# Gated mix of an S5 state space layer and a SiLU feed-forward layer: skip term from natural x, 64-row remainders in alternating order, last state tile in two halves

## The chip, the core and the metric

The kernel runs on one core of a Trainium2 chip. Its time is the device time of one execution in microseconds; the figure that counts is the median of several executions. The engines of the core are named as the profile names them: PE is the matrix engine (PEld its weight loads), DVE the vector engine, ACT the scalar engine, POOL the GpSimd engine, SP the engine that here only issues DMA transfers.

## The reference

With x of shape 2048 x 448 (tokens by channels, bf16):

```
g = sigmoid((x * gate_w).sum(-1))
Bu = x @ B_bar.T                      # complex, B_bar from Lambda, dt, B
h[t] = Lam_bar * h[t-1] + Bu[t]       # 2048 steps, 448 complex states
a = 2 * Re(h @ C.T) + x * Dskip       # the skip term is x * Dskip
b = silu(x @ w1) @ w2                 # 448 -> 1792 -> 448
out = g * a + (1 - g) * b
```

## The kernel before

**Tokens in pairs.** Token 2k is called even, token 2k+1 odd; the 1024 pairs are 8 blocks `kt` of 128. An output tile is 128 tokens of one kind by 448 channels, so there are 16 tiles, numbered `2 * kt + odd`. `XT` holds x transposed (channels on the partitions), for even tokens in its slots 0 to 3 and for odd ones in 4 to 7. 448 channels are three slots of 128 rows and a remainder of 64 rows. `XN` holds x as it lies in memory (tokens on the partitions).

**The matmuls with x.** The feed-forward layer is worked on in four chunks `c` of 512 tokens (`c // 2` is odd, `c % 2` the half of the time axis). `ffn1_mm` takes up to four blocks of 128 hidden channels at a time: for each block three matmuls over the 128-row slots (line 297), and after all blocks of the group one 64-row matmul for each (line 309). The 64-row matmuls lie alternately in the lower and the upper half of the rows, so two run side by side; the half that x isn't in is served by `XR`, a copy of the remainder in the other 64 partitions (`swap_xr`). `bu(pt, h)` does the same for the state inputs of state tile `pt` and time half `h` (lines 625 and 635). ACT takes the results out of the eight PSUM banks, which are given out in turn by `nxt`. `ffn2` (line 597) makes one output tile of the feed-forward layer, and ACT writes it times (1 - g) into the tile's place in `XN` (line 602, `bs`).

**The scan.** 448 complex states are four tiles `pt`; tile 3 holds its 64 states in one slot. `scan(pt)` on DVE combines two tokens into one step (weigh, line 655), turns the phase away by a table of cosines and sines, runs two `tensor_tensor_scan` instructions over 1024 pairs (line 662), turns back, which gives the states of odd tokens in `HS`, and then makes those of even tokens in `VE` (line 655 again). `scan3` does this for tile 3 with DMAs that swap partitions. The tables are made by POOL and DVE (`phases`, `phases2`) and by ACT (`tables`: sine, absolute value, cosine).

**The gate.** `gate` multiplies `XN` in place by a broadcast copy of `gate_w` (DVE, line 563, four instructions of 1792 columns), `gate2` sums each tile on ACT (line 571) and makes the sigmoid.

**The output stage.** `yopen` starts an output tile in a PSUM bank: five matmuls over state slots (line 754), then the skip term: three matmuls of 128 columns of `XT` with the diagonal matrices `DE` (line 756) and one of 64 rows and 64 columns (line 758). `yclose` adds the two slots of state tile 2 (line 774); DVE then multiplies by g and adds the feed-forward part (line 781), and SP stores the tile. All eight odd tiles are opened first, then closed, then the even tiles follow one by one.

**The order.** There is no scheduler. Each engine executes its instructions in the order in which the Python code records them, and `Tracker` puts semaphore waits in front of an instruction for what it reads and overwrites, by names of buffers. POOL also waits for its own previous instruction. The recorded order is the list at the end of the function (lines 805 to 862); a generator such as `s0 = scan(0)` gives its instructions piece by piece at each `run`. On SP, the DMAs stand in a queue in recorded order.

Of the kernel before, what the change touches and what calls it, by code (L numbers as in the profile page):

```python
# [7 lines left out]
ALU = mybir.AluOpType  # L8
AF = mybir.ActivationFunctionType

F32 = DT.float32
# [135 lines left out]
def gated_mix(nc, A_x, A_Lambda_re, A_Lambda_im, A_B_re, A_B_im, A_C_re, A_C_im, A_log_dt,  # L147
              A_Dskip, B_x, B_w1, B_w2, gate_w, out):
    with ExitStack() as ctx:
# [17 lines left out]
        DE = sb("DE", [128, 4, 128], BF16)  # L167
# [7 lines left out]
        OT = [sb(f"OT{i}", [128, D], BF16) for i in range(4)]  # L175
        GWB = sb("GWB", [128, D], BF16)
        JK = sb("JK", [128, 2], BF16)
# [6 lines left out]
        TMPS = [sb(f"TMP{i}", [128, D], F32) for i in range(3)]  # L184
# [4 lines left out]
        SG = sb("SG", [128, 2], F32)  # L189
        HP = sb("HP", [128, 1], F32)  # L190
# [3 lines left out]
        def bs(tile):  # L194
            return XN[:, tile * D:(tile + 1) * D]
# [64 lines left out]

        ldt_odd(0)
        ldt(XT[:, 0:4, 512:1024], x2[512:1024, 0:512], "XTe1")
        ldt_odd(1)
        XC_ALL = ["XC0", "XC1"] + [f"XC3_{q}" for q in range(4)]
# [19 lines left out]

        def ffn1_mm(c, fbs):

            odd, h = c // 2, c % 2
            hs = slice(h * 512, (h + 1) * 512)
            x0 = 4 * odd
            banks = [nxt() for _ in fbs]  # L290
            xk = XO[h] + [f"XR{h}b"] if odd else XE[h] + [f"XR{h}a"]

            for fb, bank in zip(fbs, banks):
                def mm(pe, fb=fb, bank=bank):
                    ins = None
                    for j in range(3):
                        ins = pe.matmul(ps[:, bank, :], W1E[:, j, fb * 128:(fb + 1) * 128],  # L297
                                        XT[:, x0 + j, hs], start=(j == 0), stop=False)
                    return ins
                wk = ["W1Ej0", "W1Ej1", "W1Ej2"] if fb < NFA else ["W1Ed"]  # L300
                T.op("pe", mm, reads=wk + xk, writes=[f"ps{bank}"])

            def rest(pe):
                ins = None
                for i, (fb, bank) in enumerate(zip(fbs, banks)):
                    up = (i % 2 == 1) != bool(odd)
                    p = slice(64, 128) if up else slice(0, 64)
                    x = XT[p, x0 + 3, hs] if up == bool(odd) else XR[p, hs]
                    ins = pe.matmul(ps[:, bank, :], W1E[p, 3, fb * 128:(fb + 1) * 128], x,  # L309
                                    start=False, stop=True)  # L310
                return ins
            T.op("pe", rest, reads=["W1Ea", "W1Ez"] + xk, writes=[f"ps{bank}" for bank in banks])
            return list(zip(fbs, banks))
# [153 lines left out]
        def tmp(m):  # L467
            if m < 4:
                return FP[:, 1 + m // 2, (m % 2) * 512:(m % 2) * 512 + D], f"F{1 + m // 2}"
            return TMPS[m - 4][:, :], f"TMP{m - 4}"  # L470

# [17 lines left out]
        swap_xr("dve", 0, 1)  # L489
        phases2(2)  # L490
        swap_xr("dve", 1, 0)
        swap_xr("dve", 1, 1)
# [57 lines left out]
        def side_diag():  # L550
            for j in range(4):
                T.op("dve", lambda e, j=j: e.tensor_scalar(
                    DE[:, j, :], ID[:, :], PV[:, j, 3:4], None, ALU.mult),
                    reads=["ID", "PV"], writes=[f"DE{j}"])
            yield

        def load_xn():
            ld("sp", XN[:, :].rearrange("p (k c) -> p k c", k=NKT), x2.rearrange("(k p) c -> p k c", p=128), "XN")

        def gate():  # L560
            for b in range(4):
                v = XN[:, 4 * b * D:4 * (b + 1) * D].rearrange("p (k c) -> p k c", k=4)
                T.op("dve", lambda e, v=v: e.tensor_tensor(  # L563
                    v, v, GWB[:, :].unsqueeze(1).to_broadcast([128, 4, D]), ALU.mult),
                    reads=["XN", "GW"], writes=[f"XG{b}"])
                yield

        def gate2():
            for t in range(2 * NKT):
                v = XN[:, t * D:(t + 1) * D]  # L570
                T.op("act", lambda e, t=t, v=v: e.activation(v, v, AF.Copy, accum_out=Z[:, t:t + 1]),  # L571
                     reads=[f"XG{t // 4}"], writes=[f"Z{t}", f"BS{t}"])
# [14 lines left out]
        def ffn2(c, q):  # L587
# [4 lines left out]
            bank = nxt()  # L592

            def mm(pe):
                ins = None
                for fb in range(NFB):
# [7 lines left out]
                 reads=[f"ps{bank}", "GT2"], writes=[f"BS{tile}"])  # L604
# [7 lines left out]
        def bu(pt, h):  # L612
# [7 lines left out]
            for odd, banks in ((0, be), (1, bo)):  # L620
                for m, bank in zip(ms, banks):
                    def mm(pe, m=m, bank=bank, odd=odd):
                        ins = None
                        for j in range(3):
                            ins = pe.matmul(ps[:, bank, :], bt(slice(0, 128), j, m),  # L625
                                            XT[:, 4 * odd + j, hs], start=(j == 0), stop=False)
                        return ins
                    T.op("pe", mm, reads=(["BR"] if pt == 3 else BTK[0:2]) + (XO if odd else XE)[h], writes=[f"ps{bank}"])

            def rest(pe):  # L630
                ins = None
                for m, b0, b1 in zip(ms, be, bo):
                    for odd, bank in ((0, b0), (1, b1)):
                        p = slice(64 * odd, 64 * odd + 64)
                        ins = pe.matmul(ps[:, bank, :], bt(p, 3, m),  # L635
                                        XT[p, 4 * odd + 3, hs], start=False, stop=True)
                return ins
            T.op("pe", rest, reads=(["BR"] if pt == 3 else BTK) + XO[h] + XE[h], writes=[f"ps{b}" for b in be + bo])
# [21 lines left out]
        def sc(c, pt):  # L660
            rb = c1("rr", pt).to_broadcast([128, NK])
            T.op("dve", lambda e: e.tensor_tensor_scan(G[:, c, :], rb, Q1[:, c, :], 0.0, ALU.mult, ALU.add),  # L662
                 reads=[f"Q1{c}", "rr"], writes=[f"G{c}"])

        def scan(pt):
# [6 lines left out]
            hk = [f"HS{a}", f"HS{b}"]  # L672
            cs = COS[:, pt, :].unsqueeze(1).to_broadcast([128, 2, NK])
            sn = SIN[:, pt, :].unsqueeze(1).to_broadcast([128, 2, NK])
            tk = [f"COS{pt}", f"SIN{pt}"]
            lr, li, nli = c1("lr", pt), c1("li", pt), c1("nli", pt)
            lk = ["lr", "li", "nli"]
            parts = [(0, 1), (1, 2)] if pt == 0 else [(0, 2)]
            for h0, h1 in parts:
# [3 lines left out]
                stt(u[:, 1, w], ve[:, 0, w], li, G[:, 1, w], lk + v0[0] + GK, v1[1])  # L683
                yield
            tt(Q1[:, :, :], u, cs, ALU.mult, uk[0] + uk[1] + tk, QA)
            tt(Q2[:, :, :], u, sn, ALU.mult, uk[0] + uk[1] + tk, QB)
            tt(Q1[:, 0, :], Q1[:, 0, :], Q2[:, 1, :], ALU.add, QA + QB, ["Q10"])
            tt(Q1[:, 1, :], Q1[:, 1, :], Q2[:, 0, :], ALU.subtract, QA + QB, ["Q11"])
            sc(0, pt)
            sc(1, pt)  # L690
            yield
            tt(Q1[:, :, :], G[:, :, :], cs, ALU.mult, GK + tk, QA)
            tt(Q2[:, :, :], G[:, :, :], sn, ALU.mult, GK + tk, QB)
            tt(u[:, 0, :], Q1[:, 0, :], Q2[:, 1, :], ALU.subtract, QA + QB, [hk[0]] + uk[0])
# [110 lines left out]
        for fb, bank in first:  # L805
            ffn1_act(0, fb, bank)
# [92 lines left out]
```

## Time and profile before

| what | value |
|---|---|
| median of 5 executions | 152.18 us (151.95 to 152.56) |
| profiled execution: time, span in the trace | 151.95 us, 149.9 us |
| granted PE clock | 1.000 |
| PE busy | 143.9 us (96%), 756 matmuls |
| DVE busy | 119.5 us (80%) |
| ACT busy | 81.8 us (55%) |
| POOL busy | 15.1 us (10%), none of it after 22.4 us |
| DMA | 12.30 MB |

Busy times are sums of the spans of an engine's instructions. A matmul's own span is longer than the distance to the next one, since matmuls are pipelined; its rate is read from the distance between starts. The chain of work that ended last follows the last instruction back to what released it. The timeline merges instructions of one line that follow each other into one row: start, busy time, engine, line, output and inputs, count, and in brackets how long the engine was idle before and what ended that.

### The profile page before, as it was taken

The numbers are of one execution on the slowest core, as the hardware profiler recorded it, in microseconds if no ns is written. First come the engines' busy times: TensorE is split into PE (matmuls) and PEld (weight loads), VectorE is DVE, ScalarE is ACT, GpSimd is POOL, SyncE is SP. The second block draws the span as 40 slices with busy tenths as digits, with TensorE's granted clock in tenths as the row PEclk, the third lists the DMA queues.
The fourth block names the chain that finished last, engine by engine and source line by source line (L and its number), as shares of the span: only waits on it lengthen the run. The fifth ranks groups of instructions, "written<-read, shape, count | busy, mean of one in ns | idle before, by whom it ended". The sixth has DMA issues, their size and how long they took to land.

```text
span 149.9 us, 1958 instructions
## 1 busy us (share of the span) xinstructions
PE 143.9 (96%) x756; PEld 64.8 (43%) x763; DVE 119.5 (80%) x148; ACT 81.8 (55%) x130; POOL 15.1 (10%) x20
## 2 busy tenths in 40 slices
PE   6999899999999999999999999999999999999992
PEld 2443233333354533334554333345555555555550
DVE  1573898719999999999999999999999992196441
ACT  1269969577999996988994556652131300000000
POOL 7039990000000000000000000000000000000000
PEclk9999999999999999999999999999999999999999
DMA  4998797998943003011000000000000000044211
GB/s 130 295 242 193 158 215 141 334 381 220 187 53 85 0 0 70 0 42 33 0 0 0 0 0 0 4 0 0 0 0 0 4 0 0 0 145 162 66 61 61
DMA packets 22976, 12.30 MB, mean 82 GB/s; under 512 B 16180, under 2 KB 22456, under 8 KB 22968
## 3 DMA queue, kind: packets, MB, share of 16 engines
q1 hardware_dynamic: 22388, 11.23, 29.5%
q10 hardware_dynamic: 580, 0.95, 2.2%
q8 instruction: 6, 0.10, 0.3%
q14 instruction: 2, 0.02, 0.0%
HBM read 6.15 MB, written 1.84 MB: 53 GB/s over the span
## 4 chain that ended last, share of the span: by engine, by line
PE 82%; ACT 12%; DMA 2%; issue 1%; DVE 0%
PE ps L597 25%; PE ps L297 16%; PE ps L625 12%; PE ps L754 11%; ACT AT L333 5%; PE ps L774 5%; PE ps L322 3%; PE ps L309 3%; ACT XN L571 3%; PE ps L635 3%; DMA CO<-in_A_x_dram 2%; PE ps L756 2%; ACT COS L461 2%; PE ps L758 1%; ACT SIN L456 1%; PE ps L373 1%
## 5 line engine op out<-in xcount | busy, mean ns | idle before, releaser
L597 PE MATMUL ps<-W,AT 128*128 128x448 bf16 x224 | 43.1, 353 | 0.3 <-ACT AT L333 0.3
L297 PE MATMUL ps<-XT,W1E 128*128 128x512 bf16 x142 | 33.5, 380 | 0.7 <-issue 0.5
L333 ACT ACTIVATE AT<-ps 128x1024 bf16<-128x1024 f32 (+1 forms) x32 | 27.2, 917 | 6.6 <-PE ps L309 6.6
L597 PEld LDWEIGHTS ps<-W,AT 128*128 128x128 bf16 x224 | 21.6, 98 | 21.1 <-ACT AT L333 0.7
L297 PEld LDWEIGHTS ps<-XT,W1E 128*128 128x128 bf16 x147 | 13.2, 98 | 19.8 <-issue 4.4
L781 DVE SCALAR_TENSOR_TENSOR OT<-ps,GT,XN 128x448 bf16<-128x448 f32 x16 | 10.4, 680 | 12.8 <-PE ps L774 12.7
L602 ACT ACTIVATE XN<-ps,GT 128x448 bf16<-128x448 f32 x16 | 9.6, 631 | 16.3 <-PE ps L597 16.3
L625 PE MATMUL ps<-XT,BT 128*128 128x512 bf16 x70 | 16.1, 379 | 0.8 <-ACT AT L333 0.7
L662 DVE TENSOR_TENSOR_SCAN G<-P,Q 128x1024 f32<-128x1024 f32 x6 | 13.4, 2274 | 0.0
L641 ACT ACTIVATE VE<-ps 128x1024 bf16<-128x1024 f32 (+1 forms) x8 | 7.4, 921 | 7.4 <-PE ps L635 7.4
L625 PEld LDWEIGHTS ps<-XT,BT 128*128 128x128 bf16 x72 | 6.7, 97 | 9.9 <-issue 2.0
L571 ACT ACTIVATE XN<-XN 128x448 bf16<-128x448 bf16 x16 | 9.0, 563 | 0.0
L754 PE MATMUL ps<-CO,HS 128*128 128x448 bf16 x40 | 8.9, 354 | 0.0
L754 PE MATMUL ps<-CO,VE 128*128 128x448 bf16 x40 | 8.9, 352 | 0.0
L655 DVE SCALAR_TENSOR_TENSOR HS<-VE,P,G 128x512 bf16<-128x512 bf16 (+1 forms) x8 | 7.8, 1015 | 0.1
L309 PE MATMUL ps<-XT,W1E 64*128 64x512 bf16 x25 | 7.8, 382 | 0.0
L309 PE MATMUL ps<-XR,W1E 64*128 64x512 bf16 x24 | 7.6, 382 | 0.0
L655 DVE SCALAR_TENSOR_TENSOR VE<-HS,P,G 128x1024 bf16<-128x1024 bf16 x6 | 7.4, 1281 | 0.1
L563 DVE TENSOR_TENSOR XN<-XN,GWB 128x1792 bf16<-128x1792 bf16 x4 | 4.1, 1085 | 4.1 <-DMA XN<-in_A_x_dram 4.1
L643 ACT ACTIVATE HS<-ps 128x1024 bf16<-128x1024 f32 (+1 forms) x8 | 7.4, 922 | 0.0
L655 DVE SCALAR_TENSOR_TENSOR G<-VE,P,HS 128x1024 f32<-128x1024 bf16 (+1 forms) x4 | 7.3, 1814 | 0.1
L655 DVE SCALAR_TENSOR_TENSOR G<-HS,P,VE 128x2048 f32<-128x2048 bf16 x3 | 7.0, 2350 | 0.1
(98 smaller groups left out, 167.0 us busy)
## 6 DMA issues: line engine op xcount, KB each, us to landing
XN<-in_A_x_dram SPq DMA_DIRECT2D x1, 1792.0 KB, 9.9
out_dram<-OT SPq DMA_DIRECT2D x16, 112.0 KB, 1.7
W<-in_B_w_dram SPq DMA_DIRECT2D x1, 1568.0 KB, 13.8
W1E<-in_B_w_dram ACTq DMA_DIRECT2D x3, 224.0 KB, 6.0
W1E<-in_B_w_dram SPq DMA_DIRECT2D x1, 672.0 KB, 8.7
HS<-HS SPq DMA_DIRECT2D x4, 128.0 KB, 2.3
W1E<-in_B_w_dram SPq DMA_DIRECT2D x2, 224.0 KB, 4.8
CO<-in_A_x_dram ACTq DMA_DIRECT2D x1, 256.0 KB, 4.0
```

Source lines behind the costliest of these rows:

```text
L297: ins = pe.matmul(ps[:, bank, :], W1E[:, j, fb * 128:(fb + 1) * 128], XT[:, x0 + j, hs], start=(j == 0), stop=False)
L309: ins = pe.matmul(ps[:, bank, :], W1E[p, 3, fb * 128:(fb + 1) * 128], x, start=False, stop=True)
L333: T.op("act", lambda e: e.activation(a[:, fb:fb + n, :], ps[:, bank:bank + n, :], AF.Silu), reads=[f"ps{bank + i}" for i in range(n)], wri ...
L571: T.op("act", lambda e, t=t, v=v: e.activation(v, v, AF.Copy, accum_out=Z[:, t:t + 1]), reads=[f"XG{t // 4}"], writes=[f"Z{t}", f"BS{t}"])
L597: ins = pe.matmul(ps[:, bank, 0:D], a[:, fb, q * 128:(q + 1) * 128], W2[:, fb, :], start=(fb == 0), stop=(fb == NFB - 1))
L602: T.op("act", lambda e: e.activation(bs(tile), ps[:, bank, 0:D], AF.Copy, scale=GT[:, 2, tile:tile + 1]), reads=[f"ps{bank}", "GT2"], writ ...
L625: ins = pe.matmul(ps[:, bank, :], bt(slice(0, 128), j, m), XT[:, 4 * odd + j, hs], start=(j == 0), stop=False)
L655: T.op("dve", lambda e: e.scalar_tensor_tensor(o, a, s, b, ALU.mult, ALU.add), reads=reads, writes=writes)
L662: T.op("dve", lambda e: e.tensor_tensor_scan(G[:, c, :], rb, Q1[:, c, :], 0.0, ALU.mult, ALU.add), reads=[f"Q1{c}", "rr"], writes=[f"G{c}"])
L754: ins = pe.matmul(ps[:, bank, 0:D], state(kt, odd, m), CO[:, m, :], start=(m == 0), stop=False)
L774: ins = pe.matmul(ps[:, bank, 0:D], state(kt, odd, m), CO[:, m, :], start=False, stop=(m == YB[-1]))
L781: T.op("dve", lambda e: e.scalar_tensor_tensor(o[:, :], ps[:, bank, 0:D], GT[:, 1, tile:tile + 1], bs(tile), ALU.mult, ALU.add), reads=[f" ...
```

## The change

1. The skip term is no longer made from `XT` and diagonal matrices. POOL multiplies `XN` in place by `DB`, a broadcast copy of `Dskip` (`skip`, four instructions of 1792 columns), and `yopen` adds the product with one 448-column matmul by the identity matrix. `DE` and `side_diag` go. As `XN` now keeps the product to the end, the gate products go to other buffers (`xg`: parts of `CO`, `OT` and `TMPS`), and the feed-forward parts of the tiles go to parts of `IOTA`, of `FP` and of `BT` (`bs`).
2. `ffn1_mm` and `bu` take the 64-row matmuls last and first in turn (`half`), so that those of two groups stand next to each other. `ffn2` sets the turn back.
3. `scan(2)` runs in two time halves, with 512 pairs to an instruction; the second half starts from the last value of the first. The output stage takes the eight tiles of the first time half to the end, then the other eight; `yout` (the DVE instruction and the store) is recorded apart from `yclose`, between the pieces of the second half of `scan(2)`.
4. Moves: the broadcast load of `gate_w`, and that of `Dskip`, are issued early on ACT's queue; `XN` is loaded in two halves, one before and one after the last transposing loads of x; two of the three remaining `swap_xr` copies go from DVE to POOL, behind the first two skip products; the first table set (`t0`) is recorded behind the rest of the first chunk's evacuations.

```diff
         def bs(tile):
-            return XN[:, tile * D:(tile + 1) * D]
+            kt, odd = tile // 2, tile % 2
+            if odd:
+                return BT[:, :, :].rearrange("p j n -> p (j n)")[:, kt * D:(kt + 1) * D]
+            v = (FP[:, 0, :] if kt > 3 else IOTA[:, :]).bitcast(BF16)
+            return v[:, (kt % 4) * D:(kt % 4 + 1) * D]
...
+        for dst, src, key in ((GWB, gate_w, "GW"), (DB, A_Dskip, "DB")):
+            ld("act", dst[:, :], row(src).partition_broadcast(128).rearrange("p o n -> p (o n)"), key)
         ldt_odd(0)
         ldt(XT[:, 0:4, 512:1024], x2[512:1024, 0:512], "XTe1")
+        load_xn(0)
         ldt_odd(1)
+        load_xn(1)
...
+            for part in (rests, mains) if rf else (mains, rests):
+                part()
+            half[0] = not rf
...
         phases2(1)
-        swap_xr("dve", 0, 1)
         phases2(2)
         swap_xr("dve", 1, 0)
-        swap_xr("dve", 1, 1)
...
+        def skip():
+            for b in range(4):
+                v = XN[:, 4 * b * D:4 * (b + 1) * D].rearrange("p (k c) -> p k c", k=4)
+                T.op("pool", lambda e, v=v: e.tensor_tensor(
+                    v, v, DB[:, :].unsqueeze(1).to_broadcast([128, 4, D]), ALU.mult),
+                    reads=[f"XN{b // 2}", "DB"], writes=[f"XD{b}"])
+                yield
...
-                 reads=[f"ps{bank}", "GT2"], writes=[f"BS{tile}"])
+                 reads=[f"ps{bank}", "GT2"], writes=[f"BS{tile}"] + (bsk(tile) if kt % 4 == 0 and (h == 0 or not odd) else []))
...
+            if cut:
+                for h in range(2):
+                    for f in (weigh, turn, back, even):
+                        f(h, h + 1)
+                        yield
+                return
...
-                for j in range(3):
-                    ins = pe.matmul(ps[:, bank, j * 128:(j + 1) * 128], XT[:, 4 * odd + j, xr], DE[:, j, :],
-                                    start=False, stop=False)
-                return pe.matmul(ps[:, bank, 384:D], XT[p, 4 * odd + 3, xr], DE[p, 3, p], start=False, stop=False)
+                tile = 2 * kt + odd
+                return pe.matmul(ps[:, bank, 0:D], ID[:, :], XN[:, tile * D:(tile + 1) * D], start=False, stop=False)
...
+        run(ffn1(0, NFA))
         run(t0)
-        run(ffn1(0, NFA))
         bu(0, 0)
...
-        run(g1)
+        run(g1, 2)
+        run(g0, 2)
         run(s0, 1)
         run(s3, 2)
+        run(g1)
+        swap_xr("pool", 0, 1)
+        swap_xr("pool", 1, 1)
...
         run(coef)
+        run(g0)
...
-        run(s2)
+        run(s2, 4)
...
+        done = []
+        for kt in range(4):
+            for odd in (1, 0):
+                done.append(yclose(*yopen(kt, odd)))
+        run(s2, 1)
+        yout(*done.pop(0))
+        run(s2, 1)
+        while done[2:]:
+            yout(*done.pop(0))
+        run(s2, 1)
+        while done:
+            yout(*done.pop(0))
+        opened = [yopen(kt, 1) for kt in range(4, 8)]
+        run(s2, 1)
+        for kt in range(4, 8):
+            opened.append(yopen(kt, 0))
+            done.append(yclose(*opened.pop(0)))
+        while opened:
+            done.append(yclose(*opened.pop(0)))
+        while done:
+            yout(*done.pop(0))
```

`weigh`, `turn`, `back` and `even` are the pieces of the old `scan` with bounds `h0, h1` on the time axis; the other scans call them as before. In the second half the scan's initial value is `G[:, c, 511:512]`.

## The prediction

> **What bounds the kernel now.** First the page's slices: PE is busy at 7 to 9 tenths in all but the first and last; DVE has a dip in slice 9 and is nearly free in slices 34 and 35; POOL stops after slice 6.
>
> ```profile
> PE   6999899999999999999999999999999999999992
> ...
> DVE  1573898719999999999999999999999992196441
> ...
> POOL 7039990000000000000000000000000000000000
> ```
>
> Then the chain that ended last: PE has 82% of it, ACT 12%, DVE nothing. PE reaches the output stage at 119.13 and its last matmul ends at 146.98; one DVE instruction and the store follow. So PE bounds it, and DVE has room. How much room the waits and DVE's timeline tell: DVE waits 4.15 us for `XN`, works without a gap from 33.10 to 124.51, and then waits 6.01 us for PE.
>
> ```profile
> 33.10 4.09 DVE L563 TENSOR_TENSOR XN<-XN,GWB 128x1792 bf16<-128x1792 bf16 x4 [4.15 <-DMA XN<-in_A_x_dram]
> ...
> 100.65 2.35 DVE L655 SCALAR_TENSOR_TENSOR G<-VE,P,HS 128x2048 f32<-128x2048 bf16 x1
> ...
> 122.03 2.48 DVE L655 SCALAR_TENSOR_TENSOR VE<-HS,P,G 128x1024 bf16<-128x1024 bf16 x2
> 130.53 5.72 DVE L781 SCALAR_TENSOR_TENSOR OT<-ps,GT,XN 128x448 bf16<-128x448 f32 x9 [6.01 <-PE ps L774]
> ```
>
> **PE: 64-row remainders.** PE's timeline, one group of `ffn1_mm`:
>
> ```profile
> 58.03 2.76 PE L297 MATMUL ps<-XT,W1E 128*128 128x512 bf16 x12
> 60.72 0.39 PE L309 MATMUL ps<-XT,W1E 64*128 64x512 bf16 x1
> ...
> 60.95 0.38 PE L309 MATMUL ps<-XT,W1E 64*128 64x512 bf16 x1
> ...
> 61.26 1.04 PE L297 MATMUL ps<-XT,W1E 128*128 128x512 bf16 x3
> ```
>
> Twelve matmuls take 2.76 us, the last of them 0.38, so they start 0.216 apart. Group to group is 3.23 us for fourteen such steps (12 and two pairs), which make 3.02: each excursion to 64 rows costs 0.21. In the recorded order there are 22 excursions before, 11 after (first chunk 2 to 1; the stage with `bu(0)`, `bu(3)` and `ffn1(1)` 8 to 4; `bu(1)` and `bu(2)` 2 to 1 each; `ffn1(2)` and `ffn1(3)` 4 to 2 each): 11 x 0.21 = 2.3 us.
>
> Up to `bu(1)` at 51.78 five merges lie (1.05). Moving `t0` takes away PE's wait of 0.72 at 19.02, but `ffn1(1)` still waits for the `XR` copy on DVE (behind `phases2`, it ended at 24.06 and should end near 23.9), so of all before it only about 0.2 is kept; three merges follow (0.63), and ACT, released earlier in the group with remainders first, no longer holds the second half of `ffn2(0)` (0.26). So 1.1 there, and six merges later (1.26): PE could begin the output stage at 116.7. A group with remainders first needs its four banks at once; by ACT's timeline each was free before PE comes, the closest the bank of the copies of line 648, free at 26.5 for 27.2.
>
> **PE: skip.**
>
> ```profile
> 119.13 1.11 PE L754 MATMUL ps<-CO,HS 128*128 128x448 bf16 x5
> 120.08 0.33 PE L756 MATMUL ps<-DE,XT 128*128 128x128 bf16 x3
> 120.34 0.20 PE L758 MATMUL ps<-DE,XT 64*128 64x64 bf16 x1
> 120.47 1.12 PE L754 MATMUL ps<-CO,HS 128*128 128x448 bf16 x5
> ```
>
> Skip takes 120.08 to 120.47, 0.40 with the slower start behind it; a 448-column matmul takes 0.19 ((120.08 - 119.13) / 5). 16 x 0.21 = 3.4 us saved. The stage becomes 16 x 8 x 0.19 = 24.3 and would end at 141.0. The last four closes then stand 0.38 apart and DVE needs 0.64 each (5.72 / 9), so its last instruction would end at 142.4, where before it was 147.69: 5.3 us faster, 146.9, were PE all.
>
> **DVE.** `skip` puts POOL beside DVE. What that does the first 21 us show:
>
> ```profile
> 8.23 0.24 DVE L409 TENSOR_TENSOR P<-P,PV 128x4 f32<-128x4 f32 x2 [0.28 <-ACT P L412]
> ...
> 9.91 1.03 DVE L409 TENSOR_TENSOR P<-P 128x4 f32<-128x4 f32 x2
> 12.03 1.23 DVE L451 SCALAR_TENSOR_TENSOR FP<-G,FP 128x1024 f32<-128x1024 f32 x1 [1.09 <-POOL G L446]
> ```
> ```profile
> 9.70 1.16 POOL L444 TENSOR_SCALAR FP<-IOTA,P 128x1024 f32<-128x1024 f32 x1 [5.49 <-DVE P L409]
> 10.95 1.05 POOL L446 TENSOR_SCALAR G<-FP 128x1024 f32<-128x1024 f32 x1
> 12.16 2.08 POOL L444 TENSOR_SCALAR Q<-IOTA,P 128x1024 f32<-128x1024 f32 x1 [0.17 <-POOL G L446]
> ```
>
> Two DVE instructions of four columns, 0.24 elsewhere, take 1.03 and end just behind POOL's instruction from 9.70 (10.86); POOL's at 12.16 takes 2.08 because DVE's at 12.03 is in front. Such instructions exclude each other whole, and POOL gets in after the DVE instruction in progress. Nearly all that DVE does in the scans reads two operands from SBUF as these do, so each product costs DVE its full length.
>
> That length, P, no row shows. Below: the one-operand row, 1.05 us for 1024 columns, scaled to 1792 is 1.83. [...] I take 3.93, since the products have two operands and the row has one. Two 64-row copies of 512 columns move to POOL behind the second product, an estimated 0.53 each by the same row: 1.1.
>
> The sum on DVE. ACT now does the first chunk's evacuations to about 19.2, then `t0` (3.29, from 14.58 to 17.87), so `bu(0,0)` is out at 24.3; DVE's two weighs (2.66 + 1.52, by their starts from 24.77) end at 28.5. Before, they ended at 28.95 and DVE then waited for `XN`; now its first half is loaded ahead of the last transposing loads (issued near 19.3) and there by then. From 33.10 to 100.65, where scan 2 starts, DVE worked 67.55 without a gap; `DE` goes (0.65). So scan 2 starts at 28.5 + 66.9 + 4 x 3.93 + 1.1 = 112.2 instead of 100.65. POOL's first product covers the one wait left (for ACT's evacuation of `bu(0,1)`, near 31.7).
>
> Halves: by the half-size rows (weigh and even 2.66 each, turn 4.45, with scans of 1.15 as half of 2274 ns, back 3.15) one half is 12.9, two are 25.8 instead of 23.9. The first half is done at 125.1, but PE would want it for its second tile near 119.
>
> **What waits for DVE on the way.** `scan3` keeps `FP` slot 0 until its last instruction (71.53 + 1.28 = 72.8 before; now 28.5 + 39.05 + 16.8 = 84.4). ACT must write the results of `ffn2(1)` there; queued behind are the evacuations of `bu(2)`. `bu(2,1)` needs those banks, free at about 86.6, and PE is there at 81.5: 5.1 us of wait, so the output stage starts at 121.8. In it the second tile waits for DVE (125.1), and the eighth is closed at 134.9; DVE does weigh, one output, turn, five, back, two, even: 18.1, to 143.2, without waiting; then eight outputs, 5.1, and 0.3 for PE's last closes: 148.65. Before, this was 147.69: 0.95 later. From there on the store and the end stay (149.9 - 147.7 = 2.2). Span 150.8, execution 151.95 + 0.95 = 152.9, and as the median lies 0.23 above that execution, 153.1.
>
> **Loads.** `gate_w` and `Dskip` are issued on ACT between its table load (ends 4.5) and its next instruction at 7.99: hidden. Their bytes and 0.9 MB of `XN` now precede the last loads of odd x (landed at 23.9 and 24.4), needed by `bu(0,1)` near 27.2. At the 381 GB/s of the slice with the most traffic 1.1 MB are 3 us, so PE may wait 0.3, at worst 2; DVE is behind POOL then, and the end is not moved. `W2` is issued as late as before (23.6) with fewer bytes ahead. ACT's gate sums need the third product with `gate_w` near 44.9; DVE should have it near 44.6.
>
> **Rivals.** (1) *The product is shorter.* The end follows 153.1 + 4 (P - 3.93) until PE sets it, near P = 2.4. It decides at P = 3.7, where the time is that of before; at 3.3 it is 150.6, at the row's 1.83 it is 146.9. For it: POOL's only rows are this fast, the operands are bf16. Against: none has two operands. (2) *PE gets late as well*: groups with remainders first wait for banks, or the loads of odd x slip by 2 us and more; added to the wait at `bu(2,1)` this passes the closes on to the end, 154.5 to 156. For: PE's last close (146.8) is only 1.9 before DVE's end. (3) *The merged remainders save nothing*, if the cost is per pair and not per change of rows: 2.3 us back on PE, of which about 1 reaches the end: 154. Against: between the two pairs above there is only 0.23.
>
> **How the numbers follow.** Main case 46%, 152.0 to 154.2 with P between 3.65 and 4.2; rival 1 36%, 147 to 151.7; rival 2 12%; rival 3 6%. 0.3% (0.46 us) is what a measurement can tell. Main and rival 2 and 3 above 152.64: 0.46; main between 151.72 and 152.64 with rival 1's edge: 0.14; rival 1: 0.40. The range takes in most of rival 1 and half of rival 2: 147.8 to 155.2, and 152.0 to 154.2 for the main case.
>
> **What would show it.** Right: four POOL rows of 3.5 to 4.1 us, DVE rows beside them longer by as much, scan 2 starting near 112, ACT waiting for DVE at its evacuation of `ffn2(1)`, PE waiting near 81 to 87, DVE in the chain's end; fourteen steps to the group with one change of rows; output tiles 1.51 apart. Wrong: DVE rows beside POOL no longer than elsewhere, or scan 2 before 107.

## Result, and the profile after

The changed kernel takes 152.56 us in the median of 22 executions (150.99 to 154.05), the kernel before 152.25 (151.82 to 153.13, 43 executions): the ratio is 1.0005, 95% interval 0.9988 to 1.0022. The forecast was 153.1, slower by 0.6%; measured is no difference. The profiled execution took 151.68 us with a span of 149.7 (before 151.95 and 149.9). Here and below, a ratio and its interval leave out executions more than 1.5% above the fastest of their kernel, while medians and ranges take in all. The changed kernel scatters more than the kernel before, in step with the clock granted to PE: of its 23 executions with the profiled one, the 12 with 0.995 of the clock or more average 152.03, the other 11, with 0.978 to 0.989, 152.85.

The page of the changed kernel, its slices and the engines and lines of the chain that ended last:

```profile
PE   6999959699999999999999799999999998999990
...
DVE  1563785958999999999999999999999999999974
...
POOL 7029990069939920000000000000000000000000
...
DVE 56%; PE 16%; SPq 13%; issue 7%; DMA 5%; ACT 1%; DVEq 0%
```

The bound has changed hands: DVE has 56% of the chain, where PE had 82%. It is not DVE's alone, though: at 124.15 PE waits 0.61 us for DVE, from there on PE works without a gap and the chain is PE's, and near the end DVE waits 0.81 us for PE. The two are nearly tied. (The shares of SPq and DMA lead back from DVE's row at 34.20 to the last loads of x. POOL held that row until 35.53, longer than the loads did; the chain doesn't show that.) DVE's hollow near the end (slices 34 and 35) is gone; PE has new hollows in slices 6 and 8 (18.7 to 22.5 and 26.2 to 29.9 us) and a small one in slice 23. POOL works on to slice 15.

DVE's timeline of the changed kernel:

```profile
29.88 2.21 DVE L585 TENSOR_TENSOR CO<-XN,GWB 128x1792 bf16<-128x1792 bf16 x2
34.20 2.40 DVE L696 SCALAR_TENSOR_TENSOR G<-VE,P,HS 128x1024 f32<-128x1024 bf16 x1 [2.12 <-ACT HS L684]
36.64 4.97 DVE L696 SCALAR_TENSOR_TENSOR HS<-VE,P,G 128x512 bf16<-128x512 bf16 x2
...
45.34 4.60 DVE L693 TENSOR_TENSOR Q<-HS,COS 128x2048 bf16<-128x2048 bf16 x1
49.86 4.60 DVE L693 TENSOR_TENSOR Q<-HS,SIN 128x2048 bf16<-128x2048 bf16 x1
...
110.90 1.28 DVE L696 SCALAR_TENSOR_TENSOR G<-VE,P,HS 128x1024 f32<-128x1024 bf16 x1
...
144.41 0.69 DVE L851 SCALAR_TENSOR_TENSOR OT<-ps,GT,BT 128x448 bf16<-128x448 f32 x1 [0.81 <-PE ps L841]
145.01 2.57 DVE L851 SCALAR_TENSOR_TENSOR OT<-ps,GT,FP 128x448 bf16<-128x448 f32 x4
```

and POOL's over the same stretch:

```profile
31.20 8.85 POOL L593 TENSOR_TENSOR XN<-XN,DB 128x1792 bf16<-128x1792 bf16 x2 [8.41 <-DVE CO L585]
40.19 1.90 POOL L230 COPY XR<-XT 64x512 bf16<-64x512 bf16 x2
44.55 8.82 POOL L593 TENSOR_TENSOR XN<-XN,DB 128x1792 bf16<-128x1792 bf16 x2 [2.47 <-DVE OT L585]
```

Read the two side by side. `Q<-HS,COS` takes 1.22 us where POOL is still; here it and its neighbour take 4.60. The first of them starts at 45.34, while the third product (recorded from 44.55) works, and runs only when that has ended (48.86). A row on either engine contains the wait for the other. So the true length of a product is read from the end of the DVE instruction in front of it to its own end: the first goes from 32.09 (the end of the gate products) to 35.53, 3.44 us; the second from 36.61 (the end of the row at 34.20) to 40.05, again 3.44; the other two likewise. Scan 2 starts at 110.90 and DVE's last instruction ends at 147.58, where before it was 147.69.

PE's timeline of the changed kernel, at the loads, in a pair of `ffn1_mm` groups, at `bu(2,1)`, and at the output stage:

```profile
18.46 1.46 PE L660 MATMUL ps<-XT,BT 128*128 128x512 bf16 x6
21.69 1.46 PE L660 MATMUL ps<-XT,BT 128*128 128x512 bf16 x6 [1.77 <-issue]
...
29.80 0.61 PE L672 MATMUL ps<-XT,BT 64*128 64x512 bf16 x4 [1.38 <-DMA XT<-in_A_x_dram]
...
62.44 0.39 PE L339 MATMUL ps<-XT,W1E 64*128 64x512 bf16 x1
...
62.67 0.38 PE L339 MATMUL ps<-XT,W1E 64*128 64x512 bf16 x1
...
62.88 0.38 PE L339 MATMUL ps<-XT,W1E 64*128 64x512 bf16 x1
...
63.10 0.38 PE L339 MATMUL ps<-XT,W1E 64*128 64x512 bf16 x1
...
63.64 5.13 PE L326 MATMUL ps<-XT,W1E 128*128 128x512 bf16 x23 [0.16 <-issue]
...
85.40 0.61 PE L672 MATMUL ps<-XT,BT 64*128 64x512 bf16 x4 [0.76 <-ACT FP L634]
...
120.73 1.11 PE L828 MATMUL ps<-CO,HS 128*128 128x448 bf16 x5
121.67 0.35 PE L830 MATMUL ps<-XN,ID 128*128 128x448 bf16 x1
...
124.15 0.55 PE L841 MATMUL ps<-CO,VE 128*128 128x448 bf16 x2 [0.61 <-DVE VE L696]
```

The four pairs of two groups follow each other 0.22 us apart: one excursion where there were two. The skip term is one matmul of 0.19. Both savings are there. But PE waits in the odd half of `bu(0,0)` until 21.69 and in the remainders of `bu(0,1)` until 29.80, for transposed loads of x that landed at 20.3 and 21.6 (before 18.4 and 19.6) and at 29.3 and 29.7 (before 23.9 and 24.4). (For the first wait the profile names no releaser, only "issue"; PE started at 21.69, just behind the landing.) And ACT waits for DVE, as forecast, at its evacuation of `ffn2(1)`; ACT's timeline:

```profile
77.84 1.77 ACT L567 ACTIVATE TMPS<-XC,P 128x448 f32<-128x448 bf16 x3
83.14 2.21 ACT L634 ACTIVATE FP<-ps,GT 128x448 bf16<-128x448 f32 x4 [3.53 <-DVE VE L696]
```

PE, itself late by then, loses less than 1 us to this (its row at 85.40 waits 0.76).

### The profile page after: what moved, and what is told of

The parts are those of the page before. It is cut to its first block, busy times and chain, and to the rows that moved or that the text cites. A ratio compares the mean times of both kernels' runs of the same rounds, so it can differ in the third digit from the quotient of the medians.

```text
span 149.7 us, 1886 instructions
## 1 busy us (share of the span) xinstructions
PE 139.0 (93%) x708; PEld 63.7 (43%) x715; DVE 131.1 (88%) x158; ACT 82.2 (55%) x130; POOL 34.3 (23%) x26
## 4 chain that ended last, share of the span: by engine, by line
DVE 56%; PE 16%; SPq 13%; issue 7%; DMA 5%; ACT 1%; DVEq 0%
DVE Q L693 21%; SPq L221 12%; PE ps L828 9%; DVE G L730 7%; DVE G L696 7%; DMA XT<-in_A_x_dram 5%; DVE VE L696 4%; DVE HS L693 3%; DVE HS L696 3%; PE ps L841 3%; DVE CO L575 3%; DVE FP L696 2%; PE ps L660 2%; PE ps L830 2%; DVE OT L851 2%
## 5 line engine op out<-in xcount | busy, mean ns | idle before, releaser
L593 POOL TENSOR_TENSOR XN<-XN,DB 128x1792 bf16<-128x1792 bf16 x4 | 17.4, 4346 | 11.2 <-DVE CO L585 8.4
L634 ACT ACTIVATE BT<-ps,GT 128x448 bf16<-128x448 f32 x8 | 5.1, 634 | 15.5 <-PE ps L629 15.5
L696 DVE SCALAR_TENSOR_TENSOR HS<-VE,P,G 128x512 bf16<-128x512 bf16 (+1 forms) x10 | 11.7, 1210 | 0.2
L696 DVE SCALAR_TENSOR_TENSOR G<-VE,P,HS 128x1024 f32<-128x1024 bf16 (+1 forms) x5 | 8.6, 1720 | 3.6 <-ACT HS L684 3.5
L730 DVE TENSOR_TENSOR_SCAN G<-P,Q 128x1024 f32<-128x1024 f32 (+1 forms) x6 | 11.3, 1919 | 0.0
L693 DVE TENSOR_TENSOR Q<-HS,SIN 128x1024 bf16<-128x1024 bf16 (+1 forms) x5 | 7.9, 1575 | 0.1
L693 DVE TENSOR_TENSOR Q<-HS,COS 128x1024 bf16<-128x1024 bf16 (+1 forms) x5 | 7.9, 1572 | 0.0
L693 DVE TENSOR_TENSOR Q<-G,COS 128x2048 bf16<-128x2048 f32 (+1 forms) x4 | 7.0, 1754 | 0.1
L693 DVE TENSOR_TENSOR Q<-G,SIN 128x2048 bf16<-128x2048 f32 (+1 forms) x4 | 7.0, 1750 | 0.0
L339 PE MATMUL ps<-XT,W1E 64*128 64x512 bf16 x25 | 6.7, 379 | 0.0
```

Of the source, the lines that this page charges most:

```text
L593: T.op("pool", lambda e, v=v: e.tensor_tensor(v, v, DB[:, :].unsqueeze(1).to_broadcast([128, 4, D]), ALU.mult), reads=[f"XN{b // 2}", "DB" ...
L693: T.op("dve", lambda e: e.tensor_tensor(o, a, b, op), reads=reads, writes=writes)
L696: T.op("dve", lambda e: e.scalar_tensor_tensor(o, a, s, b, ALU.mult, ALU.add), reads=reads, writes=writes)
L730: T.op("dve", lambda e, c=c, init=init: e.tensor_tensor_scan(G[:, c, w], rb, Q1[:, c, w], init, ALU.mult, ALU.add), reads=[f"Q1{c}", "rr", ...
```

## Experiments

The kernel before had medians of 152.3 to 152.4 us beside these runs. Each ratio is to it. Three questions: do PE's savings exist, what do POOL's products cost, and what do the loads cost. "Loads as before" means that the broadcasts and all of `XN` are issued on SP behind the last transposing loads of x.

### Part 2 alone, on the kernel before

The edit takes `ffn1_mm` and `bu` with their alternating order into the kernel before:

```diff
+            for part in (rests, mains) if rf else (mains, rests):
+                part()
+            half[0] = not rf
```

> The kernel before with part 2 alone (64-row matmuls last and first in turn); the whole result is computed. Theory: each change of row count costs 0.1 us on PE, 11 excursions of 0.21 us go, so the output stage starts 1.7 to 2.3 us earlier (116.8 to 117.4 instead of 119.13) and, since PE sets the end, the time is 149.9 to 150.6 us. Rival (groups with remainders first wait for their four banks as long as they save): 152 us, with new waits of PE for ACT. Rival (the cost is per pair, not per change): 152 us, with no wait.

Measured: 150.78 us (150.42 to 151.49), ratio 0.9914 (0.9884 to 0.9945). The merged remainders are worth 1.6 us by the medians and 1.3 by the ratio, less than the prediction's 2.3, and the time is a little above the 149.9 to 150.6 expected; the profiled execution lost some of the gain to a wait of 1.30 us for a load of x. The rivals in which the remainders save nothing are out.

### Products on DVE

```diff
-                T.op("pool", lambda e, v=v: e.tensor_tensor(
+                T.op("dve", lambda e, v=v: e.tensor_tensor(
                     v, v, DB[:, :].unsqueeze(1).to_broadcast([128, 4, D]), ALU.mult),
```

> The changed kernel with its four products on DVE instead of POOL, at the same places of the program; the whole result is computed. Theory (POOL's products keep DVE's two-operand instructions out for their full 3.44 us each): DVE gives 4 x 1.09 = 4.4 us for 13.8, scan 2 starts near 101.5 instead of 110.9, the wait at the evacuation of ffn2(1) goes, PE sets the end again with its 3.7 us of waits for transposing loads kept: output stage from about 119.9, time 149.6 us (149.2 to 150.2). Rival (DVE's long rows beside POOL have another cause, or PE is late for other reasons): 152.5 us or more, as DVE has 4.4 us more to do.

Measured: 151.03 us (149.59 to 152.97), ratio 0.9887 (0.9823 to 0.9951). Scan 2 starts at 101.64, as expected, 9.3 us earlier than in the changed kernel; a product takes 1.08 on DVE and its successor starts 1.0 behind it. But of those 9.3 us the time falls by only 1.5 by the medians and 1.8 by the ratios, and stays above the 149.2 to 150.2 expected: PE still begins the output stage at 120.32, because it waits 1.80 us for the last loads of odd x, and near 20 us for the first ones, as in the changed kernel, and now the chain that ended last is PE's (61%, DVE 2%). POOL's products were hiding a second loss.

### Loads as before

```diff
-        for dst, src, key in ((GWB, gate_w, "GW"), (DB, A_Dskip, "DB")):
-            ld("act", dst[:, :], row(src).partition_broadcast(128).rearrange("p o n -> p (o n)"), key)
         ldt_odd(0)
         ldt(XT[:, 0:4, 512:1024], x2[512:1024, 0:512], "XTe1")
-        load_xn(0)
         ldt_odd(1)
+        for dst, src, key in ((GWB, gate_w, "GW"), (DB, A_Dskip, "DB")):
+            ld("sp", dst[:, :], row(src).partition_broadcast(128).rearrange("p o n -> p (o n)"), key)
+        load_xn(0)
         load_xn(1)
```

> The changed kernel with its loads of gate_w, Dskip and x where they stood in the kernel before (on SP's queue, behind the last transposing loads of x); the whole result is computed. Theory (the early broadcast loads and the first half of XN hold up the transposing loads: odd x lands at 20.3 to 21.6 and 29.3 to 29.7 instead of 18.4 to 19.6 and 23.9 to 24.4, and with it the first gate product at 29.9 instead of 28.5): PE's waits of 1.9 and 1.8 us go, the first gate product starts at 28.5 to 28.9, DVE's chain and the end are 1.0 to 1.4 us earlier: 151.1 to 151.6 us. Rival (DVE then waits for XN, which comes as late as 29.9): 152.5 us.

Measured: 155.5 us (154.82 to 157.57), ratio 1.0198 (1.0163 to 1.0233). The theory fell: I had expected a gain. The transposed loads did land early (24.3 and 25.1), but DVE pays; its timeline here:

```profile
28.04 0.75 DVE L696 SCALAR_TENSOR_TENSOR HS<-VE,P,FP 128x512 bf16<-128x512 bf16 x1
33.78 2.22 DVE L585 TENSOR_TENSOR CO<-XN,GWB 128x1792 bf16<-128x1792 bf16 x2 [4.99 <-DMA XN<-in_A_x_dram]
```

Everything on DVE moves by those 3.9 us (33.78 against 29.88): scan 2 starts at 114.79. With the products on POOL, DVE has no room left. In this profile its delay reaches the end by way of `FP`: ACT waits for DVE there, and PE for ACT. PE's timeline:

```profile
89.30 1.04 PE L672 MATMUL ps<-XT,BT 64*128 64x512 bf16 x4 [3.81 <-ACT FP L634]
90.27 5.03 PE L660 MATMUL ps<-XT,BT 128*128 128x512 bf16 x12
```

The twelve matmuls take 5.03 us instead of 2.76, at a granted clock of 0.51 from 88 to 92 us ("Broadcasts later" below shows the same), and from 89.30 on PE works to the end without a gap. The profiled execution is the longest of the five (157.57, granted clock 0.978; the others had 0.987 to 0.989). So the early loads together are worth 2.9 us at the end (155.5 against 152.56); how much of it is DVE's delay and how much PE's slow stretch, this run doesn't separate.

### POOL with one operand

This kernel multiplies by 1 instead of by `Dskip`, so its skip term is x; it leaves `Dskip` out.

```diff
-                T.op("pool", lambda e, v=v: e.tensor_tensor(
-                    v, v, DB[:, :].unsqueeze(1).to_broadcast([128, 4, D]), ALU.mult),
+                T.op("pool", lambda e, v=v: e.tensor_scalar(v, v, 1.0, 0.0, ALU.mult, ALU.add),
```

> The changed kernel with POOL's products replaced by a multiplication by 1 (one operand; Dskip is left out, so the skip term is x). [...] Rival (the length comes from the width or from bf16): runs stay near 3.4 us, time 152.5 us.

Measured: 151.21 us (148.51 to 153.3), ratio 0.9836 (0.9809 to 0.9862). POOL's timeline and then DVE's:

```profile
33.49 2.43 POOL L593 TENSOR_SCALAR XN<-XN 128x1792 bf16<-128x1792 bf16 x1 [11.06 <-DVE CO L585]
36.07 2.46 POOL L593 TENSOR_SCALAR XN<-XN 128x1792 bf16<-128x1792 bf16 x1 [0.15 <-POOL XN L593]
```
```profile
43.82 2.70 DVE L692 TENSOR_TENSOR Q<-HS,COS 128x2048 bf16<-128x2048 bf16 x1
46.44 2.69 DVE L692 TENSOR_TENSOR Q<-HS,SIN 128x2048 bf16<-128x2048 bf16 x1
```

Read as above, from the end of the DVE instruction in front, a product takes 1.55 us: 34.37 to 35.92 for the first. So the rival, whose runs stay near 3.4 us, is out. DVE's rows take 2.70 instead of 4.60: longer than the 1.22 of a still POOL by 1.48, about the length of POOL's instruction. So the exclusion holds for one operand on POOL too; the product with two operands is 2.2 times as long (3.44 against 1.55; the instruction is another one as well, `tensor_tensor` for `tensor_scalar`). The loads were late here too: the first gate product starts at 32.16. The eight executions with 0.998 of the clock or more have a median of 150.4, 2.1 below the rival's 152.5; the other twelve, with 0.984 to 0.989, one of 152.65.

### Products on DVE and loads as before

Both edits together, and then also scan 2 whole, with the output order of the kernel before:

```diff
-        scan(2, True)
+        scan(2)
...
+        opened = [yopen(kt, 1) for kt in range(8)]
+        for o in opened:
+            yout(*yclose(*o))
+        for kt in range(8):
+            yout(*yclose(*yopen(kt, 0)))
```

> The changed kernel with its products on DVE and its loads where they stood before; the whole result is computed. Theory (PE sets the end once DVE is free of POOL's products; PE's waits for the transposing loads go; gate products start near 33.8, which DVE can afford now): scan 2 starts near 105, output stage near 117.3, 24.4 us long, time 147.3 us (146.8 to 148.2). Rival (the late gate products stop ACT and PE in the stage from 36 to 46 us, or DVE is still last): 150 us or more.

> The changed kernel with its products on DVE, its loads where they stood before and scan 2 whole with the output order of before; the whole result is computed. Theory: scan 2 from 105 to 129, output stage from 117.3, odd tiles closed at 129.4, even ones to 141.8, DVE's last output at 142.5 right behind PE (the last closes are 1.51 apart, not 0.38): 146.7 us (146.2 to 147.6), about 0.5 below the same kernel with halves. Rival (PE waits for whole scan 2): 148.5 us or more.

Measured: 147.61 us (147.59 to 147.65), ratio 0.9691 (0.9651 to 0.973), and 146.97 us (146.62 to 147.58), ratio 0.9653 (0.961 to 0.9697). Both as expected; the second beats both kernels by 5.3 us or more, and what it keeps of the change are the two PE parts, the products (on DVE), the two copies on POOL and `t0` behind the first chunk. The chain that ended last and PE's timeline in the second:

```profile
PE 78%; ACT 15%; DMA 3%; issue 1%; DVE 0%; ACTq 0%
```
```profile
117.50 1.11 PE L828 MATMUL ps<-CO,HS 128*128 128x448 bf16 x5
118.45 0.35 PE L830 MATMUL ps<-XN,ID 128*128 128x448 bf16 x1
118.64 1.11 PE L828 MATMUL ps<-CO,HS 128*128 128x448 bf16 x5
```

A tile is opened in 1.14 us, six matmuls of 0.19. DVE waits 3.41 us for `XN` and 5.0 for PE in the output stage: the loads cost nothing here on DVE, as it has room. The same edit of the loads thus gains 3.4 us with the products on DVE (151.03 to 147.61) and loses 2.9 with them on POOL.

### Scan 2 whole, in the changed kernel

The edit shown last, alone.

> The changed kernel with part 3 undone: scan 2 whole, all eight odd tiles opened, then closed, then the even ones; the whole result is computed. Theory (DVE is last; the halves cost it 2 us of work but let outputs start before scan 2 ends): scan 2 from 110.9 to 134.8, all banks are held by the odd tiles until DVE's first output at 135.4, then eight even tiles of 1.51 us, DVE ends near 148.3 instead of 147.6: 153.2 us (152.6 to 153.8). Rival (the halves are what makes the change bearable, outputs pile up): 155 us or more. Rival (they only cost): 151 us.

Measured: 155.2 us (153.95 to 156.43), ratio 1.0162 (1.0082 to 1.0243). The time is the rival's, but its reason isn't shown: in this profile DVE has 0% of the chain that ended last. PE's remainders of `bu(0,1)` started at 32.44 instead of 29.80, behind loads of x that the edit doesn't touch, and what followed was slow for another reason, which the next run shows more plainly: the twelve matmuls behind took 5.22 us, at a granted clock of 0.50 from 32 to 38. How much of the 2.6 us is due to the halves stays open. Where PE sets the end, the halves cost 0.64 us (147.61 against 146.97).

### Broadcasts later

```diff
-        for dst, src, key in ((GWB, gate_w, "GW"), (DB, A_Dskip, "DB")):
-            ld("act", dst[:, :], row(src).partition_broadcast(128).rearrange("p o n -> p (o n)"), key)
         ldt_odd(0)
         ldt(XT[:, 0:4, 512:1024], x2[512:1024, 0:512], "XTe1")
+        for dst, src, key in ((GWB, gate_w, "GW"), (DB, A_Dskip, "DB")):
+            ld("sp", dst[:, :], row(src).partition_broadcast(128).rearrange("p o n -> p (o n)"), key)
         load_xn(0)
         ldt_odd(1)
```

> The changed kernel with its two broadcast loads on SP's queue behind the first three transposing loads of x, the first half of XN early as in the change; the whole result is computed. Theory (the two broadcasts in the first 13 us hold up the transposing loads by 2 us): first odd x lands near 18.4 to 19.6, PE's wait of 1.9 us before the odd half of bu(0,0) goes, the first gate product starts near 28.8 instead of 29.9, the end follows by 1.1 us: 151.4 us (151.0 to 151.8) and the times scatter less. Rival (the loads' landing times vary by themselves, the broadcasts have no part): 152.5 us.

Measured: 154.16 us (153.79 to 154.47), ratio 1.012 (1.0081 to 1.0159). The theory fell again. The first loads of odd x are back at 18.8 and 20.0, but the last, now behind both broadcasts and half of `XN`, landed at 31.2 and 31.7. PE's timeline, and then stretches of the same kernel (busy time and instructions of each engine, granted PE clock, DMA share, GB/s):

```profile
31.75 1.04 PE L672 MATMUL ps<-XT,BT 64*128 64x512 bf16 x4 [4.37 <-DMA XT<-in_A_x_dram]
32.72 4.44 PE L660 MATMUL ps<-XT,BT 128*128 128x512 bf16 x12
```
```profile
30.00:34.00 4.00, 2.25 (x8) 0.62 (x9) 1.97 (x2) 0.00 (x0) 2.89 (x1) 0.50 1.02 269
34.00:38.00 4.00, 4.00 (x15) 1.63 (x14) 0.00 (x0) 1.83 (x2) 3.86 (x2) 0.73 1.08 372
38.00:42.00 4.00, 3.95 (x22) 1.54 (x21) 3.71 (x3) 3.33 (x6) 3.45 (x3) 1.00 0.74 156
```

The wait is 4.37 us, and it isn't all. The twelve matmuls behind it take 4.44 us where they take 2.76: the clock granted to PE is half until 36.2. Two prices are paid for one late load, and only the first is seen in the waits. In slices of half a microsecond to one, the half clock lasts 6.8 us here, from 29.3 (1.9 after the wait began) to 36.2 (4.4 after it ended). In the 3.4 us before 29.3, half that length, PE had worked 1.5 us.

### One load moved at a time

To price each of the two moves of loads without a late DVE, both start from the 146.97 us version. First the half of `XN`, then the broadcasts:

```diff
         ldt(XT[:, 0:4, 512:1024], x2[512:1024, 0:512], "XTe1")
+        load_xn(0)
         ldt_odd(1)
...
-        load_xn(0)
         load_xn(1)
```
```diff
+        for dst, src, key in ((GWB, gate_w, "GW"), (DB, A_Dskip, "DB")):
+            ld("act", dst[:, :], row(src).partition_broadcast(128).rearrange("p o n -> p (o n)"), key)
         ldt_odd(0)
         ldt(XT[:, 0:4, 512:1024], x2[512:1024, 0:512], "XTe1")
         ldt_odd(1)
-        for dst, src, key in ((GWB, gate_w, "GW"), (DB, A_Dskip, "DB")):
-            ld("sp", dst[:, :], row(src).partition_broadcast(128).rearrange("p o n -> p (o n)"), key)
```

> The version with the products on DVE, the loads as before and scan 2 whole (146.97 us), with one load moved: the first half of XN ahead of the last two transposing loads of odd x, as in the changed kernel. Nothing on DVE or POOL gets longer. Theory now (a wait of PE for a load is paid in full[...]): the last odd loads land near 28 to 29 instead of 24.8, PE waits 1.5 to 3 us for them near 27, the time is 148.5 to 150.5, with executions that show a granted clock near 0.987 at the upper end. Rival, the prediction's step (the loads are hidden, PE waits 0.3): 147.0 to 147.5, clock 1.0.

> The same version (146.97 us) with the other load moved: the two broadcasts early on ACT's queue as in the changed kernel, XN behind the transposing loads as before. Theory: BT lands about 1.7 us later, the first odd loads of x near 20.5 to 21.5 instead of 19.2 to 20.0, PE waits 1.5 to 2 us at the odd half of bu(0,0) near 19.5, and the last odd loads near 26 cause no further wait; 148.3 to 149.3. Rival (hidden, between ACT's table load and its next instruction): 146.7 to 147.3.

Measured: 147.94 us (147.6 to 148.82), ratio 0.9692 (0.9642 to 0.9741), 1.0 us above its start; and 148.15 us (147.77 to 149.13), ratio 0.9723 (0.9669 to 0.9777), 1.2 above. Both are below what the theory named (148.5 and 148.3 at least) and above the rival (147.5 and 147.3 at most): the loads are not hidden, and each costs about 1 us, known to some tenths (four executions of each, the ranges just apart). The profiled execution with early broadcasts is its longest, 149.13; its stretches show why (columns as above):

```profile
18.00:22.00 4.00, 1.72 (x9) 0.62 (x8) 3.29 (x4) 3.94 (x5) 3.82 (x3) 1.00 0.94 188
22.00:26.00 4.00, 4.00 (x15) 1.10 (x14) 1.51 (x2) 1.40 (x3) 1.95 (x2) 0.57 1.17 210
26.00:30.00 4.00, 3.95 (x22) 1.69 (x23) 2.98 (x4) 3.03 (x5) 0.61 (x1) 1.00 0.93 295
```

PE waited 2.28 us, less than the 3.4 us that the theory of the other move named, and still went to half clock from 22.4 to 25.8. The other three executions had 0.999 or more and took 147.77 to 148.32. So the same kernel paid the second price in one execution of four. The one-operand kernel, which has the loads of the changed kernel, shows the same behind a wait of 2.06 us at the same place: six matmuls take 2.72 us instead of 1.46 (columns as above).

```profile
18.00:22.00 4.00, 2.31 (x11) 0.87 (x9) 3.36 (x4) 3.94 (x6) 3.82 (x3) 1.00 0.90 166
22.00:26.00 4.00, 3.62 (x12) 1.01 (x12) 1.51 (x2) 1.14 (x1) 0.43 (x1) 0.57 1.09 276
```

### Half of XN late, in the changed kernel

```diff
-        load_xn(0)
         ldt_odd(1)
+        load_xn(0)
         load_xn(1)
```

> The changed kernel with the first half of XN moved back behind the transposing loads; broadcasts stay early, the products on POOL. Theory (DVE sets the end, so the first gate product does): XN's first half lands near 31 to 31.5 instead of 27.9, the first gate product starts there instead of at 29.88, the end moves with it by 1.2 to 1.7, less what PE no longer waits; 153.0 to 154.2. Rival (PE's waits for the last odd loads, with the half clock behind them, are what the changed kernel loses): those loads land near 26, PE's wait of 1.4 near 28 is gone, 150.5 to 151.7.

Measured: 153.4 us (151.71 to 154.83), ratio 1.0041 (1.0018 to 1.0065), 0.8 above the changed kernel. The last odd loads landed at 26.2 and 26.7 and PE's wait for them is gone, but the first gate product started at 31.16 and scan 2 at 112.17: the theory in which a late DVE moves the end holds, and the rival is out. In the profile, DVE's delay again reaches the end by way of the later `FP` slot, which stalls PE in earnest; PE's timeline:

```profile
86.68 1.04 PE L672 MATMUL ps<-XT,BT 64*128 64x512 bf16 x4 [3.61 <-ACT FP L634]
87.65 3.81 PE L660 MATMUL ps<-XT,BT 128*128 128x512 bf16 x12
```

Again the matmuls behind the wait run slow (3.81 instead of 2.76; granted clock 0.80 and 0.78 in the two stretches of 4 us from 84 to 92, in which it was 0.50 from 86.4 to 89.8). This wait has nothing to do with a load: PE stood idle for 3.61 us, and half the clock followed for 3.4.

## Why the prediction was wrong

The prediction's path on DVE was right, and its lengths were not. Its sum for the start of scan 2 was the first gate product + 66.9 + four products + copies. With what was measured for these terms, over all kernels with the products on POOL:

| kernel | first gate product | a product | copies | sum | measured |
|---|---|---|---|---|---|
| predicted for the change | 28.5 | 3.93 | 1.1 | 112.2 | |
| changed kernel | 29.88 | 3.44 | 0.34 | 110.9 | 110.90 |
| one operand | 32.16 | 1.55 | 0.34 | 105.6 | 105.57 |
| loads as before | 33.78 | 3.44 | 0.34 | 114.8 | 114.79 |
| half of XN late | 31.16 | 3.44 | 0.34 | 112.2 | 112.17 |
| broadcasts later | 29.78 | 3.44 | 0.34 | 110.8 | 111.20 |
| scan 2 whole | 31.05 | 3.44 | 0.34 | 112.1 | 112.45 |

The 0.34 are by how much DVE's row beside the second copy, at 41.54, is longer than its like without copies (1.09 against 0.75 us). The second instruction of the row at 36.64, beside the first copy, also takes 1.09; on the other hand the rows of 4.60 are longer by 3.38 and not by 3.44. So the sum of products and copies, 14.1 us, is firm, and its division is known to some tenths. In the last two kernels PE was so late at `bu(0,1)` that DVE waited 6.3 and 6.5 us for ACT there. POOL worked meanwhile with nothing in front of its second product, whose row is then 3.58 and 3.57; the two products ended 7.1 us behind the gate products instead of 6.9. From scan 2 to the end of DVE it was 36.7 us, with a wait of 0.81 for PE, and 36.4 without a wait by the prediction.

- **"I take 3.93" is the step that failed first.** The term was mis-sized: a product takes 3.44 us. Four of them are 1.96 less. The prediction had named 3.7 as the point from which DVE no longer makes the kernel slower, so rival 1 had the length right; its gain (150.6 at 3.3) was not measured, for the reason in the third point. No run shows 3.93 us for a product: the runs show 3.44 with two operands (`tensor_tensor`) and 1.55 with one (`tensor_scalar`). The 3.93 was nearer than the 1.83 of the one-operand row, but 14% too high, and the measured length lies on the other side of 3.7.
- **The two copies** were given 1.1 us of DVE and cost 0.34; 0.76 less.
- **"The end is not moved", said of the loads, failed.** The argument was that PE might wait but DVE would be behind POOL. Yet PE's wait in the odd half of `bu(0,0)` delays ACT's evacuation, and DVE needs that for its first weighs (25.78 instead of 24.3): the first gate product came at 29.88 instead of 28.5, 1.38 later. The broadcasts were called hidden because ACT had room for their issue; what they delayed was the landing of `BT` (14.3 for 12.6) and then of x, which the prediction looked at only for the last pair of loads.
- **What the sum makes of this:** 153.1 - 1.96 - 0.76 + 1.38 = 151.8. The prediction had added 0.23 for the median; without it the sum is 151.5, and the profiled execution took 151.68. The errors had opposite signs: with products and copies alone put right, the sum is 150.4, a gain of 1.8 us, which the loads took back. That 153.1 came within 0.6 us of the median is luck. The executions with the full clock average 152.03. The remaining half microsecond of the median is not in any step of the prediction: in the other executions PE was granted less of its clock (0.978 to 0.989). That this is the half clock behind PE's waits of 1.8 and 1.4 us is likely by the runs above: the one-operand kernel, with the same loads, shows such a stretch behind the first of these waits. No profile of the changed kernel itself does.
- **The wait of PE at `bu(2,1)`** was forecast as 5.1 us and was 0.76, since PE came later (loads) and DVE earlier (products). The output stage began at 120.73, forecast 121.8. The chain through `FP`, ACT and PE is the one forecast, and with the first gate product 1.3 us later and PE 1.6 us earlier it grew to 3.6.
- **PE's savings were nearly right.** The sum for PE alone, 146.9, was reckoned with the halves and their output order; that version with PE as the bound takes 147.61, and its output stage begins at 117.59, forecast 116.7. That the version without the halves takes 146.97 is chance. Rival 3 fell. Of rival 2 the condition came about in the changed kernel (the last loads of odd x landed 5.3 us later), its time did not; three of the experiments came near it (154.16, 155.2, 155.5), with a price that it lacked: the half clock.
- **The halves** cost 0.64 us where PE is the bound; what they are worth where DVE is late is not shown.

So the 5.3 us by which the best version beats the kernel before went in three places, by the medians: 0.6 to the halves (146.97 to 147.61), 3.4 to the loads (to 151.03), and 1.5 to POOL's products (to 152.56). By the ratios it is 0.6, 3.0 and 1.8; the step at 151.03 rests on four executions from 149.59 to 152.97. The order matters: taken first, the products cost 7.9 (147.61 to 155.5), and the early loads then give 2.9 back.

## What to carry to other kernels

Moving elementwise work from DVE to POOL relieves DVE only as far as DVE isn't made to stand still: here a product of 1.0 us on DVE held DVE for 3.44 us once it was on POOL, and DVE had the room for the 1.0. Price a moved load by the landing of every load behind it, not by the free time of the queue that issues it, and follow the first late consumer through to each engine. Cost a wait of PE at its length and, beside that, at the half clock that may follow: here 3.4 or 6.8 us of it behind waits of 2.06 to 4.37 us, and none behind one of 2.10.

## What was not expected of the hardware

- On POOL, 1792 columns of bf16 take 2.2 times as long with two operands (`tensor_tensor`) as with one (`tensor_scalar`): 3.44 against 1.55 us.
- A wait of 2.28 us was followed by 3.4 us at half clock in the profile with early broadcasts, and one of 2.06 in that of the one-operand kernel, while one of 2.10 with scan 2 whole was not; waits of 4.37 and 3.61 us were followed by half clock too, for 6.8 and 3.4 us. The matmuls behind took 4.44 and 3.81 us where twelve take 2.76, and after the short wait 2.14 where six take 1.46.
- In six profiles half the clock lasted 3.4 us (one operand, early broadcasts, half of `XN` late) or 6.8 us (loads as before, scan 2 whole, broadcasts later). In the 3.4 us ahead of it PE had worked 0.1 us (half of `XN` late), 0.8 (loads as before), 1.1 (early broadcasts), 1.4 (scan 2 whole) and 1.5 (broadcasts later). It lasted 6.8 us where PE worked 1.0 to 2.6 us in the first 3.4 of them, and 3.4 us where PE worked 3.1 (half of `XN` late) and 3.4 (early broadcasts). The changed kernel's waits of 1.77 and 1.38 us left its clock at 1.00 from 18 to 42 us.
- The first load of `BT` landed later where two loads were issued after it: in the changed kernel, with the two broadcasts issued at 3.9 and 4.5 us on ACT's queue, it was issued on SP at 3.3 and landed at 14.3; in the kernel before, without them, at 12.6.
